# A step order found anew by a free search, in an attention and gMLP kernel on one core

## The chip, the core and the metric

The kernel runs on one core of a Trainium2 chip. The core has five engines that run side by side, each through its own list of instructions in order: TensorE (PE: matmuls, with its weight loads shown apart as PEld), VectorE (DVE), ScalarE (ACT), GpSimd (POOL) and SyncE (SP), which only issues DMAs here. POOL issues DMAs as well, between its own arithmetic. Engines wait for one another by semaphores. The metric is the device time of one execution in microseconds (us).

## The reference

The inputs are q, k and v of shape (4 batches, 8 heads, 768 positions, 64) and the weights of a gMLP block. The first half is attention in which every position sees the first 4 positions (the sinks) and a window of the last 128:

```
scores = (q @ k^T) / sqrt(64);  keep = (column < 4) | (0 <= row - column < 128)
a = softmax(where(keep, scores, -1e9));  attn = a @ v        # (4, 8, 768, 64)
x = attn with heads joined                                  # (4, 768, 512)
h = gelu(x @ w_in);  u, w = first and second half of h      # 512 columns each
w = (w - mean) / sqrt(var + 1e-6) * g_ln                    # by row
s = w_sg @ w + b_sg                                         # mixes the 768 positions
out = x + (u * s) @ w_out                                   # (4, 768, 512)
```

## The kernel before

The program is one list of small steps, `STEPS`, written out in the source. Each step is a name with indices, and a loop at the end calls the function of that name for each step in turn. The function issues a few instructions on one engine. Nothing reorders them afterwards: each engine executes its instructions in the order in which the list names them, and the waits follow from the data and the buffers. A letter at a step's end names its engine where there is a choice: A for ACT, D for DVE, P for POOL.

The first index is the batch (0 to 3). The steps of one batch, with the lines of the profile:

- Loads. `LQ`, `LK` (L224) fetch q and k by POOL's DMA queue, 128 KB each, six of each in batches 1 to 3. Batch 0 is fetched instead by SP in pairs of heads (`LPQ`, `LPK`, L244, 384 KB each) and cast to bf16 by `CPQ`, `CPK`. `LVH` (L270) fetches half of v. `LW.0`, `LW.1`, `LWS.0`, `LWS.1`, `LWO` and `LB` fetch weights, all through POOL's queue. `LC` (L288) fetches the sink rows of v on SP.
- Turns. `TQ`, `TK` (L375 in batch 0, L381 in 1 and 2) transpose q and k on PE into a PSUM tile `mm`; `EQ`, `EK` copy it to `qT`, `kT`. In batch 3 the DMA does it (`DQ`, `DK`, on SP).
- Scores. `QK.b.p.g` (L482; L477 adds a mask as a bias where a fourth index is 1) computes the scores of a pair of heads p for a group g of 256 positions into a PSUM tile `sc`; `EX` (L487) takes the exponential into a tile `P`; `MK` masks it, on DVE in one instruction (L494) or on POOL in two (L497, L500). `KS`, `SK`, `SX` do the same for the sinks, `VSM` prepares their v.
- Values. `AV` (L523, L527, L530) multiplies P by v into `mm`; `NR` (L539, L540) divides by the sum and writes `x_sb`.
- First layer. x is transposed by PE and copies in batch 0 (`XT`, `XE`), by DMA in the others (`XD`). `MV` (L565) and `MU` (L606) compute the halves w and u into `sc`; `GV` (L569) and `GU` (L611) are the gelus, on ACT. `BN`, `RS`, `NM`, `Z` normalise w: statistics on DVE, the power -0.5 on POOL (L587), the scaling `Z` on ACT (L596) or DVE (L599).
- Mixing. `WT` (L618) and `WE` transpose w_sg once. `SP.b.hf.dc` (L626) multiplies by it, for a half hf of the positions and a quarter dc of the columns, into `mm`; `GT` (L631) applies g_ln and b_sg on DVE; `GM` (L636) multiplies by u, on DVE or POOL.
- Output. `OU` (L643) multiplies by w_out into `mm`; `RA` (L647) adds x; `ST` (L666) stores, on SP.

`HM.n` puts n matmuls on a zero tile (L189) ahead of the next step that takes a PSUM tile; they compute nothing that is used. `TBL` (L308) makes ACT load the table for exp or for gelu. `WARM`, `FILL`, `MASK`, `MASK0`, `IDEN`, `IDEN2`, `VSK`, `VSO` and `ZERO` set up constants; `ZERO` writes the columns of ones in the v tiles before v is loaded.

Buffers are rings: a step that takes a new one waits until the last reader of the one that many steps before is done. There are two `sc` tiles, four `mm` tiles, ten `P`, three `vt` (the gelus of w), four `gtmp` (from GT to GM) and six `ot` (from RA to ST). So the order of the list also decides which copy frees which PSUM tile for which matmul. For example, each `fresh(mm_ring, ...)` on PE needs the evacuation of the fourth `mm` tile before it.

The work of neighbouring batches is interleaved: while the gMLP block of batch 0 is under way, the scores of batch 1 and the loads of batch 2 are too.

Of the kernel before, what the change touches and what calls it, by code (L numbers as in the profile page):

```python
# [25 lines left out]
MK.0.1.0.D SX.0.1 SX.0.2 QK.0.3.1 MK.0.2.1.P GCP.D NR.0.0.0 EX.0.3.0 AV.0.0.1 AV.0.1.0 AV.0.1.1 NR.0.0.1 EX.0.3.1
QK.0.1.2 NR.0.1.0 AV.0.2.0 AV.0.3.0 EX.0.1.2 MK.0.3.1.P NR.0.1.1 QK.0.2.2 AV.0.2.1 NR.0.2.0 EX.0.2.2 TQ.1.0 NR.0.3.0
MK.0.1.2.P QK.0.3.2 AV.0.3.1 EQ.1.0.A NR.0.2.1 XT.0.0 NR.0.3.1 LWS.0 AV.0.0.2 EX.0.3.2 TBL.G AV.0.1.2 XE.0.0.D LK.1.1
XT.0.1 MK.0.2.2.D MV.0.0 XE.0.1.A LK.1.2 NR.0.0.2 MK.0.3.2.D LK.1.3 NR.0.1.2 AV.0.2.2 AV.0.3.2 LQ.1.2 NR.0.2.2 GV.0.0
MV.0.1 NR.0.3.2 LQ.1.3 BN.0.0 LWS.1 XT.0.2 GV.0.1 MU.0.1 XE.0.2.A BN.0.1 WT.0 GU.0.1 TK.1.0 MV.0.2 RS.0.1 EK.1.0.A  # L30
# [10 lines left out]
AV.1.2.1 EX.2.1.0 GM.0.1.2.P NR.1.1.1 AV.1.3.1 NR.1.2.1 QK.2.2.0 LK.3.0 QK.2.3.0 EX.2.2.0 OU.0.1 NR.1.3.1 GM.0.1.3.P
EX.2.3.0 TBL.G OU.0.2 XD.1.1 RA.0.1 GM.0.1.1.P TK.2.2 MK.2.3.0.D TQ.2.1 LVH.2.0 TQ.2.2 EQ.2.1.D MV.1.0 EQ.2.2.D LQ.3.0
EK.2.2.D LQ.3.1 VSM.2 MU.1.0 GV.1.0 MK.2.1.0.D LVH.2.1 BN.1.0 MV.1.1 GU.1.0 LQ.3.2 RA.0.2 LQ.3.3 MK.2.0.0.D MV.1.2
GV.1.1 MK.2.2.0.D LK.3.1 KS.2 LK.3.2 BN.1.1 MU.1.1 GV.1.2 LK.3.3 BN.1.2 RS.1.1 MU.1.2 GU.1.1 LQ.3.4 NM.1.1 Z.1.0.A
RS.1.2 OU.0.3 GU.1.2 TBL.E LQ.3.5 NM.1.2 Z.1.1.D SK.2.0 Z.1.4.D QK.2.0.1 Z.1.2.D Z.1.3.A QK.2.1.1 Z.1.5.D OU.0.4
# [5 lines left out]
AV.2.2.1 GM.1.1.3.P ST.0.1 NR.2.1.1 AV.2.3.1 ST.0.2 ST.0.5 GM.1.1.0.P SK.3.0 NR.2.2.1 QK.3.2.0 QK.3.3.0 NR.2.3.1
EX.3.2.0 GM.1.1.2.P SP.1.0.2 EX.3.3.0 XD.2.1 SP.1.0.3 GT.1.0.2 SX.3.0 TBL.G MK.3.3.0.D MV.2.0 GM.1.0.2.P DK.3.1
GM.1.1.1.D LK.3.4 MK.3.0.0.D OU.1.3 LVH.3.0 GV.2.0 OU.1.4 RA.1.3 LVH.3.1 OU.1.5 ST.1.3 RA.1.4 GT.1.0.3 MV.2.1 ST.1.4
MK.3.1.0.D LK.3.5 BN.2.0 GM.1.0.3.P MV.2.2 GV.2.1 BN.2.1 MU.2.1 GV.2.2 BN.2.2 RS.2.1 MU.2.0 GU.2.1 NM.2.1 RA.1.5
RS.2.2 MU.2.2 GU.2.0 NM.2.2 Z.2.4.D Z.2.5.D Z.2.0.A Z.2.1.D OU.1.0 GU.2.2 TBL.E Z.2.2.D MK.3.2.0.D OU.1.1 RA.1.0
# [20 lines left out]
def kernel(  # L76
# [124 lines left out]
    def cast(e, dst, src):  # L201
        if e == "P":
            return nc.gpsimd.tensor_scalar(out=dst, in0=src, scalar1=1.0, scalar2=1.0, op0=ALU.mult, op1=ALU.mult)
# [49 lines left out]
    def CPQ(g, e):
        return cast(e, q16.get(0)[:, S * g:S * (g + 1)], pair("q", g))

    def CPK(g, e):
        return cast(e, k16.get(0)[:, S * g:S * (g + 1)], pair("k", g))
# [457 lines left out]
```

## Time and profile before

| | |
|---|---|
| median of 3 runs | 156.04 us (155.55 to 156.66) |
| profiled execution | 156.41 us, span 154.7 us |
| instructions | 3863 |
| busy: PE, DVE, ACT, POOL | 147.4, 123.2, 99.9, 99.3 us |
| mean granted clock of TensorE | 0.997 |
| POOL's DMA queue | 64608 packets, 11.01 MB |
| SP's DMA queue | 21544 packets, 13.41 MB |

The span runs from the first to the last instruction on the core; the execution is 1.7 us longer. PE is the busiest engine. Its busy time counts overlapping matmuls once, from the first one's start to the last one's end, so short pauses between two matmuls are hidden in it. The costliest groups are the exponentials (48 EX, 953 ns each, 43.4 us on ACT) and on PE the mixing matmuls (192 matmuls of SP, 34.4 us).

### The profile page before, as it was taken

The page shows a single profiled execution, that of the slowest core. Times are in us where ns is not written, and L with a number is a line of the kernel's source. Part 1 is how long each engine was busy: PE and PEld are TensorE (multiplying, and loading weights), DVE is VectorE, ACT ScalarE, POOL GpSimd, SP SyncE. Part 2 cuts the span into 40 slices and gives each one's busy share as a digit, 9 for nine tenths or more (in the row PEclk, how much of TensorE's full clock was granted, in tenths as well). Part 3 has the DMA queues.
Part 4 walks back from the last instruction along what each step waited for, and adds up shares of the span by engine and source line. Part 5 has one row for each costly group of instructions (what it writes and reads, how often), then busy time and mean ns, then how long its engine had stood idle before and what let it go on. Part 6 is the DMA issues. An engine that isn't in the chain of part 4 may idle for free.

```text
span 154.7 us, 3863 instructions
## 1 busy us (share of the span) xinstructions
PE 147.4 (95%) x1550; PEld 94.6 (61%) x1550; DVE 123.2 (80%) x295; ACT 99.9 (65%) x117; POOL 99.3 (64%) x127
## 2 busy tenths in 40 slices
PE   6999789999999999999999999999999999999990
PEld 2455477779776776758466754585577644876530
DVE  4557789829989988897898987899799958767981
ACT  3689799699999868457987764369858022590000
POOL 4099779378999999999369769540898600400400
PEclk9999999999999999999999999999999999999998
DMA  4999999999999999999999499994610483210064
GB/s 165 295 344 157 155 195 192 169 188 190 150 144 148 186 156 173 149 154 156 157 177 252 122 277 170 192 183 58 225 72 20 86 237 112 91 72 2 0 231 177
DMA packets 86170, 24.67 MB, mean 159 GB/s; under 512 B 78660, under 2 KB 83016, under 8 KB 86152
## 3 DMA queue, kind: packets, MB, share of 16 engines
q0 software_dynamic: 64608, 11.01, 95.5%
q1 hardware_dynamic: 21544, 13.41, 32.2%
q8 instruction: 12, 0.20, 0.5%
q14 instruction: 6, 0.05, 0.1%
HBM read 24.81 MB, written 6.29 MB: 201 GB/s over the span
## 4 chain that ended last, share of the span: by engine, by line
PE 63%; POOL 18%; DMA 10%; DVE 3%; ACT 2%; issue 2%; SPq 1%; ACTq 0%
PE mm L626 17%; PE mm L643 11%; PE sc L606 10%; PE sc L565 10%; DMA v_sb<-in_v_dram 6%; POOL k L224 5%; PE sc L482 4%; DMA uT<-in_k_dram 4%; POOL q L224 4%; PE mm L523 3%; POOL wsg_gated L636 3%; PE mm L527 2%; POOL v_sb L270 2%; PE mm L381 2%; POOL P L497 2%
## 5 line engine op out<-in xcount | busy, mean ns | idle before, releaser
L487 ACT ACTIVATE P<-sc 128x1024 bf16<-128x1024 f32 (+1 forms) x48 | 43.4, 953 | 10.5 <-PE sc L482 10.4
L626 PE MATMUL mm<-wsgT,z 128*128 128x384 bf16 x192 | 34.4, 327 | 0.3 <-ACT z L596 0.3
L626 PEld LDWEIGHTS <-z 128*128 128x128 bf16 x192 | 17.6, 98 | 12.5 <-issue 0.7
L569 ACT ACTIVATE vt<-sc 128x1024 f32<-128x1024 f32 x12 | 12.3, 1026 | 18.4 <-PE sc L565 18.4
L643 PE MATMUL mm<-w_out_sb,wsg_gated 128*128 128x512 bf16 x96 | 22.7, 379 | 0.0
L631 DVE SCALAR_TENSOR_TENSOR gtmp<-mm,g_sb,b_bc 128x384 bf16<-128x384 f32 x32 | 19.0, 609 | 4.2 <-PE mm L626 4.0
L565 PE MATMUL sc<-w_in_sb,xT 128*128 128x512 bf16 x96 | 22.2, 379 | 0.0
L636 POOL TENSOR_TENSOR wsg_gated<-gtmp,uT 128x384 bf16<-128x384 bf16 x15 | 14.9, 1007 | 11.3 <-DVE gtmp L631 11.2
L606 PE MATMUL sc<-xT,w_in_sb 128*128 128x256 bf16 x192 | 22.1, 273 | 0.0
L497 POOL TENSOR_SCALAR_AFFINE_SELECT P<-P 128x512 bf16<-128x512 bf16 x21 | 13.7, 654 | 12.5 <-ACT P L487 12.5
L606 PEld LDWEIGHTS <-w_in_sb 128*128 128x128 bf16 x192 | 18.7, 98 | 3.0
L578 DVE BATCH_NORM_STATS2 st<-vt 128x6 f32<-128x512 f32 x24 | 15.4, 684 | 6.1 <-ACT vt L569 6.0
L540 DVE TENSOR_TENSOR x_sb<-mm,rcp 128x384 bf16<-128x384 f32 (+1 forms) x36 | 18.5, 513 | 1.2
L647 DVE TENSOR_TENSOR ot<-mm,x_sb 128x512 f32<-128x512 f32 x24 | 16.1, 683 | 2.0 <-PE mm L643 1.9
L587 POOL TENSOR_TENSOR rs<-rs,neg_half 128x4 f32<-128x4 f32 (+1 forms) x8 | 7.1, 883 | 15.9 <-DVE rs L582 14.5
L523 PE MATMUL mm<-v_sb,P 128*128 128x65 bf16 x192 | 15.9, 194 | 1.3 <-DMA v_sb<-in_v_dram 0.8
L224 POOL DMA_DIRECT2D k<-in_k_dram x18 | 16.4, 929 | 0.4 <-POOL wsg_gated L636 0.4
L224 POOL DMA_DIRECT2D q<-in_q_dram x18 | 16.5, 941 | 0.0
L523 PEld LDWEIGHTS <-P 128*128 128x128 bf16 x192 | 14.5, 97 | 3.2 <-issue 1.1
L611 ACT ACTIVATE uT<-sc 128x1024 bf16<-128x1024 f32 x12 | 12.2, 1022 | 5.1 <-PE sc L606 5.1
L643 PEld LDWEIGHTS <-wsg_gated 128*128 128x128 bf16 x96 | 9.2, 98 | 10.2 <-issue 0.3
L565 PEld LDWEIGHTS <-xT 128*128 128x128 bf16 x96 | 9.2, 98 | 10.1
(89 smaller groups left out, 249.4 us busy)
## 6 DMA issues: line engine op xcount, KB each, us to landing
out_dram<-ot SPq DMA_DIRECT2D x24, 256.0 KB, 2.3
v_sb<-in_v_dram POOLq DMA_DIRECT2D x8, 384.0 KB, 8.5
q<-in_q_dram POOLq DMA_DIRECT2D x18, 128.0 KB, 6.6
k<-in_k_dram POOLq DMA_DIRECT2D x18, 128.0 KB, 7.5
wsg_gated<-in_moe_w_sg_dram POOLq DMA_DIRECT2D x2, 576.0 KB, 8.4
w_in_sb<-in_moe_w_in_dram POOLq DMA_DIRECT2D x2, 512.0 KB, 10.1
uT<-in_q_dram SPq DMA_DIRECT2D x2, 384.0 KB, 3.1
uT<-in_k_dram SPq DMA_DIRECT2D x2, 384.0 KB
```

The source lines that it names most:

```text
L224: return nc.gpsimd.dma_start(out=dst.rearrange("p (h d) -> p h d", h=H), in_=heads(src, b, i))
L487: nc.scalar.activation(out=P.new((b, p, g))[:, :, 0:w], in_=sc_ring[b, p, g][:, :, 0:w], func=AF.Exp, scale=scale)
L497: nc.gpsimd.affine_select(out=p4[:, :, :, 0:128], in_=p4[:, :, :, 0:128], compare_op=ALU.is_ge, fill=0.0, base=0, pattern=[[0, 2], [0, 2], ...
L523: nc.tensor.matmul(av[:, il, hl, :], pt[:, hl, c:c + 128], vb[:, h, i, :], start=first, stop=False)
L540: nc.vector.tensor_mul(x_sb.get(b)[:, i0:i0 + n, 128 * p:128 * (p + 1)].rearrange("p t (h d) -> p t h d", h=2), av[:, :, :, 0:Dh], rcp[:, ...
L565: nc.tensor.matmul(hp[:, jl, :], xT[b][:, 2 * g + jl, c, :], w_in_sb[:, c, d_half:2 * d_half], start=(c == 0), stop=(c == KD - 1))
L606: nc.tensor.matmul(hp[:, dc // 2, 256 * (dc % 2):256 * (dc % 2 + 1)], w_in_sb[:, c, 128 * dc:128 * (dc + 1)], xT[b][:, 2 * g:2 * g + 2, c, :],
L626: nc.tensor.matmul(ps[:, 0:NH], z[b][:, si, 128 * dc:128 * (dc + 1)], wsgT[:, si, NH * hf:NH * (hf + 1)], start=(si == 0), stop=(si == NT ...
L631: nc.vector.scalar_tensor_tensor(out=gtmp.new((b, hf, dc)), in0=mm_ring["g", b, hf, dc][:, 0:NH], scalar=g_sb[:, dc:dc + 1], in1=b_bc[:, N ...
L636: (nc.vector if e == "D" else nc.gpsimd).tensor_mul(gated(b, hf)[:, dc, :], gtmp[b, hf, dc], uT[b][:, dc, NH * hf:NH * (hf + 1)])
L643: nc.tensor.matmul(ps, gated(b, hf)[:, dc, 128 * tl:128 * (tl + 1)], w_out_sb[:, dc, :], start=(dc == 0), stop=(dc == KU - 1))
L647: nc.vector.tensor_add(ot.new((b, t)), mm_ring["o", b, t], x_sb[b][:, t, :])
```

## The change

The list `STEPS` is replaced as a whole. The same loads are made, the same transposes by the same means, with the same buffers; 660 steps become 658, since two `HM` are gone. What differs:

- The order of nearly all steps, on every engine and in the DMA queues of POOL and SP.
- The engine of some steps. From ACT to DVE: CPK.2, EK.0.1, EK.1.0, EK.1.1, EK.1.2, EK.2.0, EK.2.1, XE.0.1, XE.0.2, WE.0, Z.0.0, Z.1.3, Z.2.0, Z.3.1, Z.3.3. From DVE to ACT: EQ.0.1, EQ.2.0, EQ.2.1, EK.2.2, WE.4, Z.0.3, Z.1.2, Z.2.2, Z.3.0. From POOL to DVE: CPK.1, CPK.3, three MK and five GM. From DVE to POOL: CPQ.2, two MK and eight GM.
- The mask by a bias is used for QK.0.2.1 where it was used for QK.0.3.0, so that MK.0.2.1 (on POOL) falls away and MK.0.3.0 (on DVE) is added.
- Warm-up matmuls: 9, 4, 1, 3, 1 and 3 become 10, 4, 3 and 1.

In all PE has 1547 matmuls (1550 before), DVE 301 instructions (295), ACT 110 of the listed ones (116), POOL 121 (123), SP 49 DMAs (49). The functions `CPQ`, `CPK`, `EQ`, `EK` and `turned` learn to work on half of a tile and `LVH` on a quarter of v; no step in the list uses either.

The parts of the new list that the prediction speaks of, with "..." for what is left out; first the start, up to the exponentials of batch 0:

```diff
-WARM LPQ.0 FILL LPK.0 LPK.1 LPQ.1 LPQ.2 LG MASK LPK.2 LPK.3 CPQ.0.A VSK LPQ.3 IDEN CPK.0.A IDEN2 MASK0 HM.9 TQ.0.0
-TK.0.0 EQ.0.0.D EK.0.0.A VSO HM.4 QK.0.0.0 ZERO CPK.1.P QK.0.0.1.1 EX.0.0.0 LVH.0.0 EX.0.0.1 QK.0.0.2.1 CPQ.1.D TK.0.1
...
+WARM LPQ.0 FILL LPK.0 IDEN LPK.1 LPQ.1 LPQ.2 LPK.2 MASK LPK.3 LPQ.3 VSK MASK0 CPQ.0.A LG CPK.0.A IDEN2 HM.10 TQ.0.0
+TK.0.0 EQ.0.0.D EK.0.0.A VSO ZERO HM.4 QK.0.0.0 QK.0.0.1.1 EX.0.0.0 CPK.1.D LVH.0.0 EX.0.0.1 MK.0.0.0.D QK.0.0.2.1
+CPQ.1.D TK.0.1 EX.0.0.2 TQ.0.1 LC CPQ.2.P EK.0.1.D EQ.0.1.A LVH.0.1 CPK.2.D HM.3 TQ.0.2 QK.0.1.0 TK.0.2 CPK.3.D
+EX.0.1.0 LQ.1.0 QK.0.1.1.1 EK.0.2.D EQ.0.2.A LQ.1.1 TK.0.3 EX.0.1.1 CPQ.3.D QK.0.2.0 MK.0.1.0.D LW.0 HM.1 TQ.0.3
+EK.0.3.A VSM.0 QK.0.2.1.1 LK.1.0 EX.0.2.0 EQ.0.3.D GTR EX.0.2.1 LW.1 AV.0.0.0 AV.0.1.0 KS.0 GCP.D NR.0.0.0 SK.0.1
...
```

The turn to batch 1:

```diff
-LK.1.4 NM.0.1 WE.0.A WT.1 GV.0.2 LK.1.5 TK.1.1 MU.0.2 LB.P EK.1.1.A BN.0.2 Z.0.0.A LK.2.0 WT.2 GU.0.2 MU.0.0 WE.1.D
-RS.0.2 WE.2.D Z.0.1.A LQ.2.0 NM.0.2 Z.0.2.A Z.0.3.D Z.0.4.D WT.3 LQ.2.1 WT.4 GU.0.0 TBL.E WE.3.D WT.5 LQ.1.4 Z.0.5.D
-TQ.1.1 QK.1.0.0 EQ.1.1.D QK.1.1.0 LQ.1.5 SP.0.0.0 WE.4.D LK.2.1 EX.1.0.0 VSM.1 SP.0.0.1 WE.5.D EX.1.1.0 LVH.1.0
...
+RS.0.1 WT.0 LQ.2.0 NM.0.1 GV.0.2 WT.1 Z.0.0.D WT.2 WE.0.D LB.P MU.0.2 Z.0.1.A BN.0.2 Z.0.2.A LQ.1.4 Z.0.3.A MU.0.0
+WE.1.D RS.0.2 GU.0.2 EK.1.0.D LK.1.4 NM.0.2 Z.0.4.D WT.3 GU.0.0 TBL.E LQ.1.5 WE.2.D WT.4 WT.5 WE.3.D QK.1.0.0 WE.4.A
+LQ.2.1 Z.0.5.D QK.1.1.0 TK.1.1 WE.5.D SP.0.0.0 LK.1.5 EK.1.1.D LVH.1.0 SP.0.0.1 EX.1.0.0 GT.0.0.0 SP.0.0.2 EX.1.1.0
...
```

The end:

```diff
-Z.3.0.D Z.3.1.A MU.3.0 Z.3.2.D Z.3.3.A Z.3.4.A Z.3.5.D RA.2.5 ST.2.5 SP.3.1.0 GU.3.0 SP.3.1.1 GU.3.1 GT.3.1.0 SP.3.1.2
-GM.3.1.0.D GT.3.1.1 SP.3.1.3 GM.3.1.1.D GT.3.1.2 SP.3.0.0 GM.3.1.2.D SP.3.0.1 GT.3.0.0 GT.3.1.3 SP.3.0.2 GT.3.0.1
-GM.3.1.3.P SP.3.0.3 GM.3.0.0.D GM.3.0.1.P GT.3.0.2 OU.3.3 GM.3.0.2.D GT.3.0.3 OU.3.4 GM.3.0.3.D RA.3.3 OU.3.0 RA.3.4
...
+Z.3.1.D NM.3.2 Z.3.2.D MU.3.0 Z.3.4.A Z.3.3.D Z.3.5.D SP.3.1.0 GU.3.0 SP.3.1.1 GU.3.1 GT.3.1.0 SP.3.1.2 GT.3.1.1
+GM.3.1.1.P SP.3.0.0 GT.3.1.2 SP.3.0.1 GT.3.0.0 GM.3.1.0.D GM.3.0.0.P SP.3.1.3 SP.3.0.2 GT.3.1.3 GM.3.1.2.D GM.3.1.3.P
+SP.3.0.3 GT.3.0.1 GT.3.0.2 GM.3.0.1.P OU.3.3 GT.3.0.3 OU.3.4 GM.3.0.3.D RA.3.3 OU.3.5 GM.3.0.2.D ST.3.3 RA.3.4 OU.3.0
...
```

More of the change, by code (lines that the diff above doesn't have):

```diff
@@ L26 @@
[L26 to L30, printed above, removed]
@@ L41 @@
[L41 to L45, printed above, removed]
@@ L51 @@
[L51 to L55, printed above, removed]
@@ L251, in LPK, with half, CPQ, CPK @@
         return load_pair("k", k, g)
[L253 to L257, printed above, removed]
+    def half(x, h):
+        return x if h is None else x[:, S // 2 * h:S // 2 * (h + 1)]
+    def CPQ(g, *how):
+        h, e = how if len(how) > 1 else (None, *how)
+        return cast(e, half(q16.get(0)[:, S * g:S * (g + 1)], h), half(pair("q", g), h))
+    def CPK(g, *how):
+        h, e = how if len(how) > 1 else (None, *how)
+        return cast(e, half(k16.get(0)[:, S * g:S * (g + 1)], h), half(pair("k", g), h))
     def LV(b, t):
@@ L269, in LVH @@
     def LVH(b, i):
+        n = 2 if VHOW[b] == "Q" else 4
+        hs = slice(n * i, n * i + n)
         return nc.gpsimd.dma_start(
-            out=v_sb.get(b)[:, 4 * i:4 * i + 4, :, 0:Dh].rearrange("p h t d -> p (h t) d"),
-            in_=v[b, 4 * i:4 * i + 4].rearrange("h (t p) d -> p (h t) d", p=128))
+            out=v_sb.get(b)[:, hs, :, 0:Dh].rearrange("p h t d -> p (h t) d"),
+            in_=v[b, hs].rearrange("h (t p) d -> p (h t) d", p=128))
     def LW(half):
@@ L414, in turned @@
         if HOW[b] in "AG":
-            return copy(e, dst.get(b)[:, S * g:S * (g + 1)].rearrange("p (i t) -> p i t", t=NT),
-                        ps16((name, b, g), NT).rearrange("p t i -> p i t"))
+            i = slice(0, 128) if h is None else slice(64 * h, 64 * h + 64)
+            return copy(e, half(dst.get(b)[:, S * g:S * (g + 1)], h).rearrange("p (i t) -> p i t", t=NT),
+                        ps16((name, b, g), NT).rearrange("p t i -> p i t")[:, i])
         return copy(e, dst.get(b)[:, 2 * d_model * g:2 * d_model * (g + 1)],
```

70 lines of the change are left out of this document (41 added, 29 removed).

## The prediction

> **What bounds the kernel now.** I read the page from the top: engines' busy time, then the slices.
>
> ```profile
> PE 147.4 (95%) x1550; PEld 94.6 (61%) x1550; DVE 123.2 (80%) x295; ACT 99.9 (65%) x117; POOL 99.3 (64%) x127
> ...
> PE   6999789999999999999999999999999999999990
> ```
>
> TensorE is busy for 95% of 154.7 us, and almost without a hole after the first ten slices. A busy PE need not be PE at its peak, so I took the starts of its instructions step by step from the timeline and measured each step by the distance to the next one: SP 0.97 us, OU 0.86, MV 1.73, MU 1.75, a transposed group of eight 0.45, AV 0.18 to 0.54, QK 0.23 to 0.32 (0.85 with a bias). With its usual distance for every step, the order from the first warm-up matmul at 1.25 us to the last OU sums to 139.4 us; it takes 149.1. Of the 9.7 us between them about 4 lie in the first 20 us, and the rest is small change (a QK costs some 0.1 us more when an SP follows). The windows by stage say the same:
>
> ```profile
> 0.00:17.50 17.50, 15.43 (x168) 7.53 (x169) 11.31 (x33) 12.98 (x17) 10.96 (x20) 1.00 1.42 229
> 27.00:62.50 35.50, 35.26 (x448) 25.89 (x445) 29.73 (x72) 30.70 (x37) 31.58 (x38) 1.00 2.05 167
> 137.40:154.70 17.30, 13.16 (x74) 6.96 (x72) 10.96 (x20) 1.94 (x2) 1.90 (x2) 0.97 0.29 108
> ```
>
> Columns: stretch, its length, then busy time of PE, PEld, DVE, ACT, POOL, the clock, the DMA share, GB/s. From 27 us on a new order can only win what PE still waits for, and PE's own list of waits is short (us in total, times, longest):
>
> ```profile
> PE mm L523 <- DMA v_sb<-in_v_dram: 0.8, 1, 0.8
> PE mm L523 <- DVE rcp L539: 0.5, 1, 0.5
> PE mm L626 <- ACT z L596: 0.3, 1, 0.3
> PE mm L381 <- DMA k<-in_k_dram: 0.2, 1, 0.2
> ```
>
> The first two lie before 21 us. So the end is set by how early PE becomes saturated plus what it loses later, and any new order is judged by these two.
>
> **The change, part by part.** I laid the new order's rows end to end by hand, engine by engine, with durations from the groups and the timeline, and compared PE's position with the old one wherever the same steps had been done. The PE work is the same: 1550 matmuls become 1547 (21 warm-ups become 18). The bias of one QK moves from a 384-wide to a 512-wide pair: +0.1 us at most, inside the slack of the start.
>
> *Warm-ups.* The first batch grows from 9 to 10. They run 0.427 us apart there, and the first transposes (5.19 us) started directly behind them, so everything after starts 0.43 us later. The four saved later are 0.22 us each and stood where PE waited for ScalarE's exponentials: worth nothing. A rule that speaks against dropping them: the Trainium skill (TensorE: Matmul & The Clock Gate, "What's actually happening") has the clock halve after a window of about 3.4 us without work. Here PE's largest hole in that stretch is 1.08 us, so by that rule too the clock stays up.
>
> *The first v load.* This chain runs through the old start:
>
> ```profile
> 8.01 0.78 POOL k L203
> 8.79 8.73 DMA v_sb<-in_v_dram
> 17.52 0.04 issue
> 17.56 0.25 PE mm L523 x3
> ```
>
> POOL's cast CPK.1 waited for its pair until 7.92 us and held back LVH.0.0; in the new order DVE makes that cast, and LVH.0.0 waits for ZERO alone (7.6 us, now 8.1). The load can land about 0.7 us earlier, at 16.8. Bounds: nothing earned if the pair loads and v merely divide the DMA engines, 0.7 if they don't; I take most of it, since v's packets began at 11.4 us, when the pair loads were nearly through. The Trainium skill (DMA: Bandwidth & Descriptors, "Queues, rings and completion order") says that a DMA engine takes turns between queues; by that, the last pair loads land later by what v gains, and the term is 0.35 worse. AV.0.0.0 then waits for what precedes it on PE: DVE now has three more casts of k and one less of q. Its chain CPK.1, MK, CPQ.1, EK.0.1, CPK.2, CPK.3, EK.0.2, CPQ.3 (casts 0.56 to 0.98, copies 0.95) ends near 15.4, so TQ.0.3 and the biased QK.0.2.1 end near 17.0. That is 0.5 before the old 17.56. But VSM.0 (0.69) now stands ahead of EQ.0.3 (0.95) and KS.0 on DVE; SK.0.1 and QK.0.3.0 behind it on PE wait until about 17.8. From there the exponentials pace PE (0.92 each), and MV.0.1 comes at 26.8 instead of 26.96. **-0.15 us.** Bounds: -1.2 (casts all at 0.56) and +0.5 (v at 17.5, casts at 0.98).
>
> *The turn from batch 0 to 1.* Here is the old order, with DVE's and PE's pieces:
>
> ```profile
> 36.29 1.01 DVE L199 COPY wsgT<-mm 128x768 bf16<-128x768 bf16 x2
> ...
> 39.01 0.54 DVE L599 TENSOR_SCALAR z<-vt,rs,nmr 128x512 bf16<-128x512 f32 x1
> ```
>
> Between BN.0.2's end (36.38) and Z.0.5 (39.55) DVE works without rest. The new order gives it EK.1.0 (a copy of 0.69) in that stretch and takes Z.0.3 (0.54) but adds WE.2 before Z.0.4. WT.3 now needs the mm buffer that EK.1.0 frees near 37.5 (a wait of 0.3), and SP.0.0.0, which needs Z.0.5 near 39.9, starts near 40.0. The old one started at 39.98 having done TQ.1.1 too (0.54 with the step to QK): 39.44 for the same work. So 0.3 behind instead of 0.15 ahead: **+0.45 us.** Bounds 0 and +0.8. Behind SP.0.0.0 on PE stand all SP and QK of batch 1; they wait with it.
>
> *Batch 1.* All loads of q, k, w_sg and v queue on POOL; while that queue was full they landed 0.85 us apart (128 KB), 2.9 (half of v), 2.8 (half of w_sg). By those steps the new sequence has LK.1.1 in at 27.9 us for TK.1.0 at 28.8, LWS.0 at 31.5 for WT.0 at 32.6, LVH.1.0 at 47.8 for AV.1.0.0 at 51.4, LQ.2.5 at 62 for TQ.2.2 at 63.8: in time, the first by under a microsecond. POOL puts MK.0.3.1, MK.0.1.2 and MK.0.2.2 (1.2 each) ahead of LWS.0; its queue is still 5 us deep then, so this costs nothing, and up to 1 us if it isn't. New waits: SP.0.1.3 needs GT.0.1.1's buffer and AV.1.1.0 needs MK.1.1.0, both late in a full DVE queue: 0.25 and 0.15. Gone: TK.2.1's second half, which the list above shows waiting for k (0.41 by its step), is moved behind OU.0.2, and small ones like it. **-0.2 us**, bounds -0.5 and +0.7.
>
> *Batch 1's normalisation.* SP.1.0.0 lost 0.54 us waiting for Z.1.3 on ScalarE behind the table load. The new one has Z.1.2 there; SP.1.1.0 stops one accumulation step (0.16) earlier. **+0.15**, bounds 0 and +0.3.
>
> *Batches 2 and 3.* Position by position I find PE within 0.3 us of the old at MV.2.0, SP.2.0.0 and MV.3.0. **0**, bounds -0.5 and +0.6; the tight places are AV.2.2.1 behind MK.2.2.2 (1.15 on DVE) and AV.3.2.1 to OU.2.2, each of whose buffers DVE frees within 0.2 us of need. On SP's queue DK.3.0 now stands behind ST.0.3 and can issue at 76.5 us, for QK.3.0.0 at 88; XD.2.0 stands behind DQ.3.2 and ST.0.2, and issues near 86 as before. POOL issues LK.3.2, LK.3.3 and LK.3.5 later than before, and DK.3.1 and DK.3.2 behind them land near 105 and 110 us, for QK.3.0.1 at 107.7 and QK.3.0.2 at 112.6: hidden, with 2 us to spare.
>
> *The tail.* The old rows:
>
> ```profile
> 143.78 1.90 POOL L636 TENSOR_TENSOR wsg_gated<-gtmp,uT 128x384 bf16<-128x384 bf16 x2 [8.72 <-DVE gtmp L631]
> 144.07 0.83 DVE L636 TENSOR_TENSOR wsg_gated<-gtmp,uT 128x384 bf16<-128x384 bf16 x1
> 145.21 5.34 PE L643 MATMUL mm<-w_out_sb,wsg_gated 128*128 128x512 bf16 x24
> 146.45 0.36 DVE L636 TENSOR_TENSOR wsg_gated<-gtmp,uT 128x384 bf16<-128x384 bf16 x1
> ```
>
> A GM on DVE takes 0.36 us alone and 0.83 beside POOL's. In the new order SP.3.1.3 is sixth, not fourth, of the last eight SP. With T for the end of the eighth, GT.3.1.3 ends at T-1.15, GM.3.1.2 at T-0.6 to T-0.3, and GT.3.0.1, whose buffer OU.3.3 takes, at T to T+0.3: OU.3.3 starts 0.15 to 0.45 late (it had no wait). GM.3.0.2 is behind RA.3.3 and ends at T+2.9 to 3.3, so OU.3.0 loses up to 0.4 more. **+0.55**, bounds +0.1 and +0.85. The final RA and store are the same.
>
> Sum: -0.15 + 0.45 - 0.2 + 0.15 + 0 + 0.55 = +0.8 us. The profiled execution took 156.41 us with a span of 154.7, so 1.7 lie around it, unchanged; 155.5 span, 157.2 by that execution. The median shown is 156.04, 0.37 less: **156.8 us**.
>
> **Rivals.**
> *It gains.* Every buffer is freed in time, the start keeps 0.7 (v at 16.8, casts at 0.56), and the old waits of 0.41, 0.54 and 0.2 vanish with the tail at +0.1: -0.7-1.15+0.1, 154.3 us. For it: DVE is busy 80%, and each wait I found is under half a microsecond. Against: DVE gets 301 instructions for 295 while ScalarE, with 65%, loses six.
> *DVE becomes the bound in batch 1 (the other side).* In 27 to 62.5 us it is busy 29.7 of 35.5, and from 38 us on at 80% or more in nearly every slice. Five copies of k and q to kT and qT move to it from ScalarE and three go back; two more x 0.7, plus MK at 0.68 where 0.55 was read, twelve times, is 1.4 + 1.6 = 3.0 us, and some 1 us of cover is there. It decides once SP.0.0.0 starts after 40.6. Together with the tail, 156.04 + 2.0 + 0.6: 158.6 us.
> *A load comes late.* LWS.0 or LK.1.1 misses PE by 1 to 2 us, because the queue drained while POOL masked: 158.2 us.
> *The clock drops at the start.* Warm-ups were 0.427 us apart before 7 us and 0.216 after; with four fewer of them a long hole could bring the slow rate back for some 4 us of matmuls: +2 at most, 158.0 us. The clock's row, 1.00 in every stretch above but the last, and holes of at most 1.08 us speak against it. By the Trainium skill's rule cited above it would take a hole of 3.4 us.
>
> **How the numbers follow.** Chances: forecast 0.50, gain 0.17, DVE bound 0.25, late load 0.06, clock 0.02. About 1% is what a measurement here can tell from no change: 154.5 to 157.6. The forecast's own range is 155.7 to 157.8, of which 0.41 of its 0.50 lies within 1%, 0.06 above and 0.03 below; the gain gives 0.10 faster and 0.07 same; the other three 0.31 slower, 0.02 same. Together 0.13, 0.50, 0.37. The range reaches from the gain to beyond the DVE case, 154.4 to 159.0, with a tenth left out on either side.
>
> **What would show it.** Right: PE still 94 to 95% busy; the v wait of 0.8 us gone; SP.0.0.0 near 40.0; a gap ahead of L643's last run; L523 beginning near 17.1. DVE rows would release more of PE's idle time than before. Wrong: MV.0.1 before 26.0 or SP.0.0.0 before 39.4 (then it gains), L626 waiting for L599 by over a microsecond (the DVE case), or L618 or L381 waiting for a DMA.

## The result, and the profile after

The changed kernel takes 157.26 us (median of 10 runs) where the kernel before takes 156.20 in the same comparison: ratio 1.0071, 95% interval 1.0044 to 1.0098. The profiled execution took 157.17 us with a span of 155.4. Two of the ten runs (159.7 and 159.8 us), and the profiled one of `lk33_first` below, were in a slower state of the chip, and every ratio here leaves such runs out. So the new order is slower by 0.7%. The forecast of 156.8 was close, but most of its terms were not: losses that it named in batch 1 and at the tail are not there, others that it did not name are, and the start came out better.

The page of the changed kernel, its engines and PE's slices:

```profile
PE 145.9 (94%) x1534; PEld 93.3 (60%) x1547; DVE 127.4 (82%) x301; ACT 95.3 (61%) x111; POOL 98.8 (64%) x125
...
PE   6998899999999999999899999998999999999980
```

PE has 94% where it had 95%, and an 8 in slices 20 and 28 where all were 9 (13 of its 1547 matmuls have no record here, so the busy time is a little low). The same three stretches as before:

```profile
0.00:17.50 17.50, 14.70 (x169) 7.14 (x171) 12.12 (x35) 12.08 (x14) 11.17 (x20) 1.00 1.55 232
27.00:62.50 35.50, 34.73 (x435) 25.27 (x437) 31.70 (x71) 25.45 (x31) 31.50 (x38) 1.00 2.01 166
137.40:154.70 17.30, 13.70 (x79) 7.49 (x77) 9.90 (x19) 1.94 (x2) 3.65 (x4) 1.00 0.25 93
```

In the middle stretch DVE is busy 31.7 us instead of 29.7 and ACT 25.5 instead of 30.7: the work moved from ACT to DVE is seen here. PE's 34.7 for 35.3 says little: some of its records are missing here, and second executions of the same two kernels (`before_again` and `after_again`, below) have it the other way round, 34.7 before and 35.0 changed:

```profile
27.00:62.50 35.50, 34.72 (x430) 25.07 (x428) 29.45 (x71) 29.77 (x36) 30.55 (x37) 1.00 2.02 164
```

```profile
27.00:62.50 35.50, 35.02 (x438) 25.02 (x435) 32.17 (x73) 25.58 (x31) 31.64 (x38) 1.00 1.96 165
```

What PE waited for (us in total, times, longest):

```profile
PE mm L469 <- DVE ks_sink L457: 0.7, 1, 0.7
PE sc L490 <- DMA kT<-k: 0.6, 1, 0.6
PE mm L634 <- ACT z L604: 0.4, 1, 0.4
PE mm L634 <- ACT wsgT L198: 0.3, 1, 0.3
```

The wait for v (0.8) is gone, and so is the one for k. In their place stand the sinks' k (KS, L457), a transposed k of batch 3 (`kT`), and a copy of w_sg on ACT (`wsgT`). With four smaller ones the list sums to 2.9 us, to 1.8 before (the first warm-up's 1.2 left out of both). In the second executions it sums to 2.9 and to 2.3, and v's wait in the kernel before is only 0.2 there.

To see where time goes I use PE's *lag*: a step's start on PE less the usual distances (from one step's start to the next one's) of all useful steps done before it. Two orders can be compared by it at any step, even where they did different work up to there. Lag of the changed kernel less that of the kernel before, in the two profiles:

| step | reached at | difference of lag |
|---|---|---|
| MV.0.1 | 26.18 us (26.96 before) | -0.98 |
| SP.0.0.0 | 38.78 (39.98) | -0.96 |
| SP.0.0.1 | 40.25 (40.97) | -0.47 |
| QK.1.0.1 | 44.48 (44.45) | -0.26 |
| OU.0.1 | 58.80 (59.46) | -0.50 |
| MU.1.2 | 71.40 (71.21) | 0.00 |
| MU.2.0 | 102.47 (101.64) | -0.23 |
| QK.3.0.1 | 108.49 (106.96) | +0.47 |
| AV.3.0.1 to the last OU | 119.28 (118.70) | +0.40 |

So the start gains a microsecond here, and it is given back at single places. The rows of three of them. First the turn to batch 1 (start, duration, engine, line):

```profile
38.02 1.28 ACT L315 ACT_TABLE_LOAD   x1
...
39.42 0.78 ACT L198 COPY wsgT<-mm 128x768 bf16<-128x768 bf16 x1
...
40.25 0.49 PE L634 MATMUL mm<-wsgT,z 128*128 128x384 bf16 x2 [0.33 <-ACT wsgT L198]
```

SP.0.0.1 takes the mm buffer that WE.4 (L198) empties. WE.4 stands behind the load of the exp table on ACT and ends at 40.20; SP.0.0.1 starts 1.47 us behind SP.0.0.0 instead of 0.97. Then QK.1.0.1:

```profile
42.50 1.32 DVE L644 TENSOR_TENSOR wsg_gated<-gtmp,uT 128x384 bf16<-128x384 bf16 x1
42.62 0.97 POOL L644 TENSOR_TENSOR wsg_gated<-gtmp,uT 128x384 bf16<-128x384 bf16 x1
...
43.74 0.68 DVE L199 COPY qT<-mm 128x1024 bf16<-128x1024 bf16 x1
```

GM.0.0.0 on DVE took 1.32 us while POOL ran a GM of its own beside it and then issued a load; the same operation takes 0.36 alone. EQ.1.1 (L199) behind it is late, and QK.1.0.1 with it. Third, the chain of waits around 60 us:

```profile
59.81 7.20 DMA xT<-x_sb
67.01 0.05 issue
67.06 1.05 PE sc L573 x4
```

XD.1.1, the DMA that transposes the second half of x, landed 7.2 us after its issue, and MV.1.1 stood for it.

### The profile page after: what moved, and what is told of

The parts are those of the page before. It is cut to its first block, busy times and chain, and to the rows that moved or that the text cites. A ratio compares the mean times of both kernels' runs of the same rounds, so it can differ in the third digit from the quotient of the medians.

```text
span 155.4 us, 3830 instructions
## 1 busy us (share of the span) xinstructions
PE 145.9 (94%) x1534; PEld 93.3 (60%) x1547; DVE 127.4 (82%) x301; ACT 95.3 (61%) x111; POOL 98.8 (64%) x125
## 4 chain that ended last, share of the span: by engine, by line
PE 53%; DMA 21%; DVE 8%; ACT 6%; POOL 5%; issue 3%; SPq 1%; DVEq 0%; ACTq 0%; POOLq 0%
PE mm L634 15%; PE mm L651 8%; PE sc L573 7%; PE sc L614 7%; DMA k<-in_k_dram 5%; DMA xT<-x_sb 5%; DMA z<-in_q_dram 4%; PE sc L490 4%; DMA vs<-in_v_dram 4%; DMA kT<-k 3%; PE mm L531 3%; PE mm L535 2%; PE mm L388 2%; PE mm L538 2%; ACT L315 2%
## 5 line engine op out<-in xcount | busy, mean ns | idle before, releaser
L634 PE MATMUL mm<-wsgT,z 128*128 128x384 bf16 x192 | 34.2, 326 | 0.7 <-ACT z L604 0.4
L634 PEld LDWEIGHTS <-z 128*128 128x128 bf16 x192 | 17.9, 98 | 12.8 <-ACT z L604 0.8
L505 POOL TENSOR_SCALAR_AFFINE_SELECT P<-P 128x512 bf16<-128x512 bf16 x19 | 12.2, 644 | 16.5 <-ACT P L495 16.5
L651 PE MATMUL mm<-w_out_sb,wsg_gated 128*128 128x512 bf16 x88 | 22.3, 379 | 0.4
L644 POOL TENSOR_TENSOR wsg_gated<-gtmp,uT 128x384 bf16<-128x384 bf16 x18 | 16.7, 939 | 8.4 <-DVE gtmp L639 8.2
L655 DVE TENSOR_TENSOR ot<-mm,x_sb 128x512 f32<-128x512 f32 x24 | 16.2, 686 | 5.1 <-PE mm L651 4.9
L502 DVE TENSOR_TENSOR P<-P,mask 128x768 bf16<-128x768 bf16 (+1 forms) x25 | 15.7, 643 | 1.5 <-ACT P L495 1.4
L531 PE MATMUL mm<-v_sb,P 128*128 128x65 bf16 x192 | 16.3, 194 | 0.0
L224 POOL DMA_DIRECT2D k<-in_k_dram x18 | 16.3, 914 | 0.0
L490 PE MATMUL sc<-qT,kT 64*128 64x128 bf16 (+1 forms) x256 | 14.9, 238 | 1.1 <-DMA kT<-k 0.6
L535 PE MATMUL mm<-v_sb,P 128*128 128x65 bf16 x160 | 15.6, 194 | 0.1
```

Source lines behind the costliest of these rows:

```text
L224: return nc.gpsimd.dma_start(out=dst.rearrange("p (h d) -> p h d", h=H), in_=heads(src, b, i))
L490: nc.tensor.matmul(sc[:, hl, c:c + 128 * ni], at(kT, b)[rows, j, p, :], at(qT, b)[rows, i:i + ni, p, :], start=not biased, stop=(not biase ...
L531: nc.tensor.matmul(av[:, il, hl, :], pt[:, hl, c:c + 128], vb[:, h, i, :], start=first, stop=False)
L535: nc.tensor.matmul(av[:, il, hl, :], pt[:, hl, c:c + 128], vb[:, h, i - 1, :], start=False, stop=(i < 2 and il == n - 1 and hl == 1))
L634: nc.tensor.matmul(ps[:, 0:NH], z[b][:, si, 128 * dc:128 * (dc + 1)], wsgT[:, si, NH * hf:NH * (hf + 1)], start=(si == 0), stop=(si == NT ...
L644: (nc.vector if e == "D" else nc.gpsimd).tensor_mul(gated(b, hf)[:, dc, :], gtmp[b, hf, dc], uT[b][:, dc, NH * hf:NH * (hf + 1)])
```

## The experiments

Two theories. *Single waits*: each loss belongs to one step that stands behind the wrong neighbour in its queue, and goes when that step is moved. *VectorE too full*: DVE has more to do and every buffer comes a little late; what is taken away at one wait is lost again at the next. A third question is whether the early start is the order's or the chance of one execution.

Step numbers and tiles are as above; the line numbers of these kernels are 5 lower than in the changed kernel (L629 is its L634).

**The start and the rest, exchanged.** Both lists were cut behind MV.0.1.

> The new list as far as MV.0.1, then what is left of the old list in its old order (the mask that the new bias replaces is left out). Theory: the new start is really about 0.9 us better (MV.0.0 to QK.1.0.0 stood 0.98 us earlier in the changed kernel, counted at equal PE work done), and all that the change loses is lost behind it. So this kernel should keep the gain: about 155.3 us where the kernel before takes 156.2, ratio 0.994. Rival 'luck of the clock': the granted clock rose at 5.1 us in the changed kernel's profile and at 7.0 in the one before, and the early start comes from that and not from the order; then 156.2, ratio 1.000. Rival 'the start is worse': 156.5 or more.

> The old list as far as MV.0.1, then what is left of the new list. Theory: it has the losses of the new order (some 1.9 us after MV.0.1) without the gain of its start: 156.2 + 1.9 = 158.1 us, ratio 1.012. Rival 'luck of the clock': the rest of the new order loses 1.1 net whatever the start: 157.3, ratio 1.007. If the new rest loses nothing by itself: 156.2.

Measured: the new start with the old rest 1.0115 (1.0074 to 1.0156), the old start with the new rest 1.0194 (1.0144 to 1.0245). The first is slower than the kernel before, as only the rival of a worse start had it, but its interval overlaps that of the changed kernel. The second is slower than either whole list, and than the 1.012 of its theory. What PE waited for in each, new start first:

```profile
PE mm L621 <- DMA wsg_gated<-in_moe_w_sg_dram: 0.9, 1, 0.9
```

```profile
PE mm L383 <- DMA k<-in_k_dram: 1.6, 1, 1.6
```

The new start had MV.0.1 1.45 us ahead of before, and lost 1.65 up to QK.1.0.0, because the old rest wants w_sg and k earlier than the new start's queue brings them. (This trace is of the fastest run, 156.55 us, and ends 0.1 us ahead of the kernel before; what the slower runs lose beyond that, no trace shows.) The old start issues LK.1.1 behind three masks on POOL (23.6 us, landing 30.7; the changed kernel 16.6 and 27.9), where the new rest has TK.1.0 at 29. So in these traces the two halves are tied together by POOL's queue, and the exchange doesn't give the price of a half.

**One wait at a time.** `WE.4` ahead of the table load:

```diff
-WT.3 GU.0.0 TBL.E LQ.1.5 WE.2.D WT.4 WT.5 WE.3.D QK.1.0.0 WE.4.A LQ.2.1
+WT.3 GU.0.0 LQ.1.5 WE.2.D WT.4 WT.5 WE.3.D QK.1.0.0 WE.4.A TBL.E LQ.2.1
```

> The changed kernel with ScalarE's copy WE.4 ahead of the load of the exp table instead of behind it. SP.0.0.1 takes the mm buffer that WE.4 frees and stood 0.49 us longer than usual behind SP.0.0.0 for it. Theory (single waits): WE.4 ends near 38.9 instead of 40.2, SP.0.0.1 follows SP.0.0.0 at 0.97 us instead of 1.47, and most of that stays to the end: 156.8 us where the changed kernel takes 157.3, ratio to the kernel before 1.004. Rival (VectorE as a whole is too full, every buffer comes a little late): the half microsecond is lost again before batch 2 and the time stays 157.2 to 157.3, ratio 1.007.

Measured: 157.25 us, 1.0059 (1.0025 to 1.0093). The wait is gone:

```profile
38.12 0.79 ACT L193 COPY wsgT<-mm 128x768 bf16<-128x768 bf16 x1
38.93 1.28 ACT L310 ACT_TABLE_LOAD   x1
...
39.00 1.79 PE L629 MATMUL mm<-wsgT,z 128*128 128x384 bf16 x10
```

But 0.68 us were lost at QK.1.0.1 (0.31 in the changed kernel's profile) and 0.87 at MV.1.1 (0.11). The time lies between the two theories, 1.004 and 1.007, and its interval holds both. The places speak for single waits: both are named waits that the changed kernel has as well, with sizes that differ from one execution to the next.

**LK.3.3 ahead of LVH.3.0.**

```diff
-GM.1.0.3.P LVH.3.0 OU.1.0 GV.2.0 OU.1.1 LK.3.3 RA.1.0
+GM.1.0.3.P LK.3.3 LVH.3.0 OU.1.0 GV.2.0 OU.1.1 RA.1.0
```

> The changed kernel with the load LK.3.3 ahead of LVH.3.0 in POOL's queue. In the changed kernel LK.3.3 landed at 103.17 us, DK.3.1 on SP's queue waited for it, and QK.3.0.1 stood 0.58 us for kT. Theory (single waits): LK.3.3 lands about 2 to 3 us earlier, the wait for kT vanishes from PE's list, QK.3.0.1 comes 0.5 to 0.7 us earlier, and that stays to the end: 156.7 us, ratio to the kernel before 1.003. Rival (VectorE as a whole is too full): QK.3.0.1 comes earlier, but AV.3.0.0 or SP.2.x takes it back: 157.2, ratio 1.007. It would be worse if LVH.3.0 then came late for AV.3.0.0 (111 us).

Measured: 1.0078 (1.0037 to 1.0119), no gain. The wait moved by one step, from QK.3.0.1 to QK.3.0.2:

```profile
116.77 0.50 PE L485 MATMUL sc<-qT,kT 64*128 64x256 bf16 x7 [0.69 <-DMA kT<-k]
```

DK.3.1 now transposed while both halves of v were loading; LK.3.5 landed 11.6 us after its issue began (8.7 in the changed kernel), and DK.3.2 waits for LK.3.5. (Only the order of events is read from this trace; `six_moves`, below, has the same move, the same 11.6 and the same wait.)

**XD.1.1 without the burst of loads beside it.** The kernel before had POOL compute there: XD.1.1 landed 4.5 us after its issue.

```diff
-NR.1.1.1 LQ.2.5 AV.1.3.1
+NR.1.1.1 LQ.2.5 GM.0.1.2.P GM.0.1.0.P GM.0.1.3.P AV.1.3.1
```

> The changed kernel with POOL's three GM of batch 0's second half (GM.0.1.2, .0, .3) moved ahead of the loads LK.3.0, LQ.3.0 to LQ.3.3, so that no load is issued while XD.1.1 transposes. XD.1.1 landed 4.5 us after its issue in the kernel before, where POOL computed beside it, and 7.2 to 7.8 in the kernels with the new order, where five loads in a row were issued beside it; MV.1.1 then stood 0.11 to 0.93 us for it. If the loads are the cause: XD.1.1 lands 4.5 to 5.2 us after its issue, near 64.8, and MV.1.1 and MV.1.0 have no wait; PE stands 0.3 to 0.9 us better at MV.1.2 than in the changed kernel and its relatives. If they are not: 7 us or more again. Time: 156.4 to 157.0 us by the theory of single waits, 157.2 by the theory that VectorE as a whole is too full (the next buffer then comes late instead).

Measured: 156.85 us in one run, which can't tell the theories apart. The landing times of the XD of batch 1 (least, median, most; the trace of before has only XD.1.1's), in the kernel before, the changed one and this one. XD.1.1's are 4.5, 7.2 and 4.1:

```profile
DMA to landing us min/median/max: 4.5/4.5/4.5
```

```profile
DMA to landing us min/median/max: 4.6/5.9/7.2
```

```profile
DMA to landing us min/median/max: 4.1/4.4/4.7
```

Here XD.1.1 was the faster of the two, and MV.1.1 has no wait. In the changed kernel it cost 0.33 us (MV.1.0 and MV.1.1), in its second trace 0.68, in we4_first, lk33_first and old_start 0.87 to 0.93, in cpk1_pool and k3_first (below) 0.49 and 0.33. That the burst of loads is the cause is shown: in the seven traces where POOL issues four loads within 3 us behind XD.1.1's issue, it landed after 7.2 to 7.8 us; in the six where POOL's next load comes 2.0 us behind or later, after 4.1 to 4.9, though a load was in flight there too. The Trainium skill (DMA: Bandwidth & Descriptors, "Queues, rings and completion order") says that a DMA engine takes turns between its queues packet by packet; the landing of 7.2 against 4.1 agrees with it.

**The same kernels again**, for the spread of the start:

> The kernel before once more, unchanged, for a second trace of its start. Three traces with the new start up to MV.0.1 (the changed kernel, new_start, we4_first) have MV.0.1 at 26.18, 25.72 and 26.41 us; two with the old start at 26.96 and 26.62. If the order makes the difference, this one has MV.0.1 at 26.6 to 27.2 again and the clock's rise may fall anywhere between 4.5 and 7 us; if the rise of the clock makes it, MV.0.1 follows the rise: at 25.7 to 26.2 when it comes near 5 us.

> The changed kernel once more, unchanged, for a second trace. By equal PE work done, MV.0.1 stood 0.98, 1.45, 0.76 and 0.24 us ahead of the first trace of before in four traces with the new start, 0, 0.34 and 0.30 in three with the old one. Theory: 0.2 to 1.2 ahead again; behind it SP.0.0.1 loses 0.5 (WE.4), MV.1.1 0.9 (XD.1.1 lands 7.2 to 7.8 us after its issue), SP.1.1.0 0.6, QK.3.0.1 0.6. If a wait is missing here, it belonged to that one execution and not to the order.

Measured: 157.19 and 157.52 us, one run each. Lag at MV.0.1 against the first trace of before: old start 0, -0.30 and -0.34; new start -0.98, -1.45, -0.76, -0.24, -0.15 and -0.48 (the changed kernel, new_start, we4_first, xd_free, after_again, and k3_first, below). The means are -0.2 and -0.7. So the new start is better by about 0.5 us on these nine traces, whose two ranges overlap, with a spread of 1.3 between executions of one order; half of the difference in the first two profiles was chance. The rise of the clock doesn't make it: in seven_moves (below) the first transposes of q still take 0.85 us, as in the kernel before, and MV.0.1 stands 1.07 ahead; in after_again they take 0.53, and it stands 0.15 ahead. The second trace of the changed kernel has SP.0.0.1 (0.50), MV.1.1 (0.68) and SP.1.1.0 (0.59) again, but at QK.3.0.1 only 0.15 instead of 0.80 (the gaps of 0.22 and 0.58 at the two OU ahead of it). That wait belonged to one execution more than to the order; QK.1.0.1's is down to 0.1. The second trace of the kernel before has such a wait of its own: inside AV.1.3.1 PE stood 0.6 us for a mask of POOL. At the last OU this execution is 0.8 us behind the first one, as far as after_again is. So a pair of traces can't price the two orders; the ten runs of each can.

**CPK.1 on POOL again.**

```diff
-QK.0.0.0 QK.0.0.1.1 EX.0.0.0 CPK.1.D LVH.0.0
+QK.0.0.0 QK.0.0.1.1 EX.0.0.0 CPK.1.P LVH.0.0
```

> The changed kernel with the cast CPK.1 on POOL, ahead of LVH.0.0, as the kernel before has it. The prediction gave the move of this cast to VectorE most of 0.7 us: LVH.0.0 is issued 1.2 us earlier and v lands 1.3 us earlier. If v's landing is what the start waits for, this kernel loses it again: LVH.0.0 issued near 8.8 and landing near 17.5 us, AV.0.0.0 at 17.5 and MV.0.1 about 0.5 to 0.9 us later than in the changed kernel; 157.9 us. If the start is paced by VectorE's casts and ScalarE's exponentials instead: AV.0.0.0 late, but SK.0.1 and MV.0.1 within 0.2 us of the changed kernel or earlier, since VectorE has one cast less ahead of KS.0; 157.2 us or less.

Measured: 157.07 us, 1.0064 (1.0030 to 1.0098), the same as the changed kernel. LVH.0.0 was issued 1.7 us later, and nothing measurable was lost by it (MV.0.1 at -0.46):

```profile
8.56 0.83 POOL L198 TENSOR_SCALAR k<-uT 128x768 bf16<-128x768 f32 x1 [5.57 <-DMA uT<-in_k_dram]
9.34 1.99 POOL L272 DMA_DIRECT2D v_sb<-in_v_dram  x1
```

v landed at 16.92, within the 16.2 to 17.3 of the kernels that issue it at 7.5 to 8.2, so the landing near 17.5 that was to be tested did not come about. In these traces its landing depends little on its issue (the earliest issue, 7.1 in new_start, landed at 15.6); my explanation, not tested, is that the pair loads of q and k (the last lands at 13.1) hold the DMA engines until then.

**All of it together.** Six moves: the three above, and three more.

```diff
-EK.0.3.A VSM.0 QK.0.2.1.1 ... AV.0.1.0 KS.0 GCP.D
+EK.0.3.A QK.0.2.1.1 ... AV.0.1.0 KS.0 VSM.0 GCP.D
...
-QK.1.3.0 GM.0.0.0.D EX.1.2.0 TQ.1.1 GM.0.0.1.P SP.0.0.3 EX.1.3.0 EQ.1.1.D LWO GT.0.0.2 QK.1.0.1 QK.1.1.1 GT.0.0.3
+QK.1.3.0 EX.1.2.0 TQ.1.1 GM.0.0.1.P SP.0.0.3 EX.1.3.0 GT.0.0.2 EQ.1.1.D LWO QK.1.0.1 QK.1.1.1 GT.0.0.3 GM.0.0.0.D
...
-GU.1.2 TBL.E NM.1.2 MK.2.0.0.D SK.2.0 Z.1.4.D Z.1.2.A QK.2.0.1
+GU.1.2 Z.1.2.A TBL.E NM.1.2 MK.2.0.0.D SK.2.0 Z.1.4.D QK.2.0.1
```

> The changed kernel with six moves of steps, one for each single wait that the traces show: WE.4 ahead of the exp table's load; GT.0.0.2 and EQ.1.1 ahead of GM.0.0.0 on VectorE (QK.1.0.1 stood 0.2 to 0.7 us for EQ.1.1); POOL's three GM ahead of the loads beside XD.1.1 (0.3 to 0.9 us); Z.1.2 ahead of the next table load (SP.1.1.0 stood 0.59 us for it); LK.3.3 ahead of LVH.3.0 (QK.3.0.1 stood 0.6 us for kT); VSM.0 behind KS.0 (SK.0.1 stood 0.9 us for KS.0). Theory (single waits): what is taken away stays away, 0.5 + 0.2 + 0.5 + 0.6 + 0.6 + 0.5 = 2.9 us less than the changed kernel: 154.4 us where the kernel before takes 156.4, ratio 0.987. Rival (VectorE as a whole is too full): other buffers come late in their place, and at most a third is kept: 156.3 to 157.0, ratio 0.999 to 1.004.

Measured: 156.06 us, 0.9963 (0.9934 to 0.9992). From 1.0071 that is 1.7 us of the 2.9 that the theory added up, more than the third that its rival allowed. The waits at SP.0.0.1, QK.1.0.1, MV.1.1 and SP.1.1.0 are gone; GM.0.0.0, away from POOL's, took 0.35 us. PE's lag is 1.28 us better than before at MU.2.0. Behind AV.3.1.0 it loses 0.8 again, since QK.3.0.2 waits for kT as in lk33_first:

```profile
PE sc L485 <- DMA kT<-k: 0.7, 1, 0.7
```

So the sixth move, LK.3.3, brings a wait to both kernels that have it without the next one, and takes one away that only two of the six traces of the new rest without it show (the changed kernel's first and old_start). The rest of that cure is to bring all k of batch 3 ahead of the second half of v:

```diff
-OU.1.2 LVH.3.1 RA.1.1 RA.1.3 MV.2.1 RA.1.2 LK.3.4 BN.2.0 LK.3.5 MV.2.2
+OU.1.2 RA.1.1 RA.1.3 MV.2.1 RA.1.2 LK.3.4 BN.2.0 LK.3.5 LVH.3.1 MV.2.2
```

> The changed kernel with LK.3.3 ahead of LVH.3.0 (as in lk33_first) and LVH.3.1 behind LK.3.5. In lk33_first and six_moves the wait for kT went from QK.3.0.1 to QK.3.0.2 (0.7 us): DK.3.1 ran at 97 us beside the loads of v, LK.3.5 landed 10.7 us after its issue instead of 7.8, and DK.3.2 waited for it. If the order of these loads in POOL's queue is the cause, LK.3.5 lands 3 us earlier here, DK.3.2 lands before 110, and neither QK.3.0.1 nor QK.3.0.2 waits for kT; PE stands 0.6 to 0.7 us better at AV.3.0.1, counted from MU.2.0. If v's second half comes late instead, AV.3.2.0 waits for it.

> The kernel six_moves with a seventh move, LVH.3.1 behind LK.3.5. six_moves took 156.06 us where the kernel before took 156.56 and lost 0.9 us ahead of QK.3.0.2, whose kT came late. Theory (single waits): that wait goes too, 155.2 us, ratio to the kernel before 0.991. Rival (another buffer comes late in its place): 156.0, ratio 0.996.

Measured: k3_first, with these two load moves alone on the changed kernel, 156.73 us in one run. LK.3.5 lands 5.8 us after its issue began, QK.3.0.2 follows without a wait. From MU.2.0 to AV.3.0.1 PE improves by 0.08; the changed kernel loses 0.62 there in its first trace, but improves by 0.03 in its second. So on its own the pair of moves removes a wait that not every execution has.

seven_moves: 154.96 us where the kernel before takes 156.25, ratio 0.9921 (0.9892 to 0.9949). It beats both kernels. The seventh move is worth what it should be: from MU.2.0 to AV.3.0.1 six_moves loses 0.71 and seven_moves gains 0.08. Its page and its stretch from 27 to 62.5 us:

```profile
PE 146.8 (96%) x1547; PEld 94.1 (62%) x1547; DVE 124.9 (82%) x301; ACT 95.1 (62%) x111; POOL 98.3 (64%) x125
...
PE   6998999999999999999999999999999999999980
```

```profile
27.00:62.50 35.50, 35.38 (x446) 25.96 (x445) 31.44 (x73) 26.18 (x31) 32.00 (x39) 1.00 2.00 173
```

This settles the rival. DVE does the same 301 instructions and is nearly as busy as in the changed kernel (82% in both, and 31.4 us of the stretch for 31.7), yet PE has 35.4 of 35.5. Of PE's own waits one line is left behind the first warm-up:

```profile
PE mm L377 <- DVE k L194: 0.4, 1, 0.4
```

The chain that ended last says it in another way, in the kernel before, the changed one and seven_moves:

```profile
PE 63%; POOL 18%; DMA 10%; DVE 3%; ACT 2%; issue 2%; SPq 1%; ACTq 0%
```

```profile
PE 53%; DMA 21%; DVE 8%; ACT 6%; POOL 5%; issue 3%; SPq 1%; DVEq 0%; ACTq 0%; POOLq 0%
```

```profile
PE 88%; DVE 4%; POOL 3%; ACT 1%; issue 1%; POOLq 0%
```

The kernel before has 37% of its chain elsewhere, half of it on POOL; the changed kernel nearly half, on landings and copies; with seven moves the chain stays on PE. Only the last is a finding: the second executions of the first two have 54% and 68% on PE, and all twelve other traces have 49 to 71, while seven_moves has 88 in its one trace.

## Why the prediction came out as it did

**The sum.** Forecast +0.8 us on the profiled execution, measured +0.76 there and +1.06 between the medians. The sign and size are right by cancellation: a start whose gain was under-priced, a tail that was over-priced, and losses that were not seen. That the total came out is luck. By one of the prediction's own signs it should have gained: SP.0.0.0 came at 38.78 us, before the 39.4 that it named. The steps behind it gave that lead back.

**Warm-ups** ("everything after starts 0.43 us later"): wrong. The rows, before and after:

```profile
5.19 0.85 PE L375 MATMUL mm<-iden,q 128*64 128x128 bf16 x12
5.92 0.85 PE L375 MATMUL mm<-iden,k 128*64 128x128 bf16 x12
```

```profile
5.40 0.53 PE L382 MATMUL mm<-iden,q 128*64 128x128 bf16 x12
5.94 0.53 PE L382 MATMUL mm<-iden,k 128*64 128x128 bf16 x12
```

q's transpose came 0.21 later, k's 0.02: it waits for the cast CPK.0, which ends at 5.87 to 5.89 in both. (That the transposes take 0.53 us for 0.85 is not the order's: with the same start they take 0.74 in xd_free and 0.85 in seven_moves.) The step that failed was to carry a delay forward without asking what the next instruction waits for.

**The start** (-0.15, bounds -1.2 and +0.5): the first pair of profiles gives -0.98, the two means over nine traces differ by about 0.5. The mechanism named, v landing earlier because its load is issued earlier, is not borne out: cpk1_pool issues it late, v lands within the range of the other new starts, and nothing is lost. Whether an early landing by itself helps stays open. Of the nine traces with the new start, those with small changes in it included, the three in which v landed by 16.3 us (new_start, the changed kernel, seven_moves) are the three furthest ahead (1.45, 0.98, 1.07); but k3_first stood 0.8 us for v and is 0.48 ahead all the same. The second part of the step holds: SK.0.1 does wait behind VSM.0 and EQ.0.3 for KS.0 (the 0.7 in PE's list). Moving VSM.0 took that wait away, but the lag at MV.0.1 with it (-0.53 and -1.07) is within the spread of the others.

**The turn** (+0.45, at WT.3 and Z.0.5): the size is right by luck, the place wrong. EK.1.0 took 0.68 on DVE as priced, but WT.3 followed MU.0.0 without a wait and SP.0.0.0 came at 38.78. The 0.49 arose at the next matmul, on ACT: I followed DVE's queue, and not WE.4, which the change moves to ACT behind the table load.

**Batch 1** (-0.2): TK.2.1's wait is gone as said (-0.36 between OU.0.0 and OU.0.1), and the loads that I forecast landed where I had them (LK.1.1 at 27.89 for 27.9, LWS.0 31.56 for 31.5, LVH.1.0 47.90 for 47.8, LQ.2.5 62.29 for 62). The waits at SP.0.1.3 and AV.1.1.0 did not come. Not seen were QK.1.0.1 (0.3 and 0.7 in two traces, 0.2 or less in the others), MV.1.1 (0.3 to 0.9), and a stop of 0.25 inside AV.1.0.1, which every trace of the new rest has and where, by the times, PE stands for POOL's mask MK.1.0.2. For the first I had the price in hand (a GM beside POOL's GM takes 0.83 or more) and used it for the tail alone. For the second I followed when SP issues its DMAs, not what POOL issues beside them.

**Batch 1's normalisation** (+0.15): SP.1.1.0 loses 0.59 where SP.1.0.0 lost 0.54, so +0.05. **Batches 2 and 3** (0): right in most traces. "DK.3.1 hidden, with 2 us to spare" was wrong in the first, where it landed late enough to cost 0.7.

**The tail** (+0.55): 0. From SP.3.1.0 to the last OU the lag doesn't change in any trace of the new order. DVE and POOL there, and then PE's output rows (L651):

```profile
144.59 0.34 DVE L644 TENSOR_TENSOR wsg_gated<-gtmp,uT 128x384 bf16<-128x384 bf16 x1
144.82 1.78 POOL L644 TENSOR_TENSOR wsg_gated<-gtmp,uT 128x384 bf16<-128x384 bf16 x2 [1.06 <-DVE gtmp L639]
144.86 1.84 DVE L639 SCALAR_TENSOR_TENSOR gtmp<-mm,g_sb,b_bc 128x384 bf16<-128x384 f32 x3
...
146.73 0.36 DVE L644 TENSOR_TENSOR wsg_gated<-gtmp,uT 128x384 bf16<-128x384 bf16 x1
```

```profile
145.81 5.34 PE L651 MATMUL mm<-w_out_sb,wsg_gated 128*128 128x512 bf16 x23
```

DVE's GM took 0.34 and 0.36, not 0.83, since they hardly overlapped with POOL's; GT.3.0.1 ended at 145.47, ahead of the need at 145.81.

**The rivals.** The forecast's rival of a full DVE is refuted by seven_moves. The gain rival was right that the start gains and that two of the old waits vanish (0.41 and 0.2; the 0.54 is 0.59 now, at SP.1.1.0). The late load came, on a smaller scale than its 1 to 2 us and at other loads: XD.1.1 and DK.3.1. The clock's row is 1.00 in all three stretches. It is so too where the first warm-ups run 0.43 us apart, so for the start the spacing says more: the warm-ups behind the first ten are 0.22 us apart, and PE did not fall back. By the Trainium skill's rule that the prediction cites, a fall would have needed an idle window of about 3.4 us; PE's longest here, ahead of SK.0.1, is 0.7 us, and the trace agrees. (The 1.08 us that the prediction gives for the kernel before runs from start to start; idle were 0.8 of it.)

## What to carry to other kernels

When PE is at 95%, a new order is priced not by how full the engines are but by the few steps whose producer stands behind a long neighbour in its own queue: a copy behind a table load, a copy behind a multiply that another engine slows, a DMA beside a burst of loads. Go through every producer that changes its engine or its neighbour, not only those on the fullest engine, and judge a repair by the place in the trace and not by one total: of the repairs that ran by themselves none showed in the time beyond its uncertainty, while seven together brought the ratio from 1.0071 to 0.9921, 1.5% less (with both intervals, 1.1 to 1.9). And take more than one trace before a start is called better, or a wait is called the order's.

## What the runs showed of the hardware

- The DMA transpose XD.1.1 on SP's queue landed 4.1 to 4.9 us after its issue in six traces where POOL's next load came 2.0 us behind it or later, and 7.2 to 7.8 in seven where four loads of 128 KB came within 3 us. DK.3.2 behaves alike: 7.3 and 7.4 us beside the second half of v (seven_moves, k3_first), 3.0 to 3.8 in the others. LK.3.5, a load, landed after 8.7, 11.6 and 5.8 us in three orders (the changed kernel, six_moves, k3_first); how much of that is the transposes beside it and how much the halves of v ahead of it in POOL's queue, no run separates.
- GM on DVE (two bf16 operands, 128x384) takes 0.34 to 0.36 us alone, 0.83 beside POOL's GM (the kernel before), 1.32 beside POOL's GM and a load issued by POOL, and up to 1.68 in we4_first. The Trainium skill (GPSIMD Engine Reference, "1. Specifications") says that POOL's interfaces to SBUF are shared with DVE, with contention for DVE instructions that have two inputs in SBUF; these rows agree with it. It is not POOL's GM alone: GM.0.1.1 took 1.06 us in the changed kernel beside nothing but the issuing of loads by POOL, and GM.0.0.0 0.35 beside such issuing in six_moves.
- The same list reaches MV.0.1 within a range of 1.3 us from one execution to the next, and behind it single waits of up to 0.8 us come and go (QK.3.0.1 in the changed kernel, AV.1.3.1 in the kernel before).
